# A table of due times, x of the first batch through DRAM, low k in three and more products of zeros in a pooled-attention and two-MLP kernel

## The chip, the cores and the metric

The kernel runs on one core of one Trainium2 chip. The metric is the device time of one execution in microseconds (us). Lower is better. The engines are PE (matmul; PEld is its weight load), DVE, ACT, POOL (GpSimd) and SP, which issues nearly all DMAs; each works through its own list of instructions in order.

## The reference

All arrays are float32. Queries are averaged in pairs (1152 to 576), then 16 heads (2 batches of 8) attend to 1152 keys, and two MLPs follow over the 1152 pooled tokens.

```python
q_pool = q.reshape(B, H, S // factor, factor, D).mean(axis=3)      # (2, 8, 576, 64)
scores = scale * np.matmul(q_pool, k.transpose(0, 1, 3, 2))        # (2, 8, 576, 1152)
attn = np.exp(scores - np.max(scores, axis=-1, keepdims=True))
attn = attn / (np.sum(attn, axis=-1, keepdims=True) + 1e-09)
x = np.matmul(attn, v)                                             # to (1152, 512)
h = x @ w_in;  x = np.maximum(0.01 * h, h) @ w_out                 # 512 -> 2048 -> 512
h = x @ w_in2; x = (h / (1.0 + np.exp(-h))) @ w_out2               # 512 -> 2048 -> 512
```

## The kernel before, in words

**Precision.** A matmul operand is a sum of a rounded high part (fp32r, made by a copy on ACT) and a low part (value minus high, a subtraction, mostly on POOL). A product of two such operands is three matmuls: high by high, low by high, high by low. q, k, x, the weights and the hidden g are all split in this way.

**Attention** (`attention`) goes over 8 pairs of heads, four of each batch. For a pair, `load` and `load_v` issue the DMAs of k, q and v (`L455`), POOL adds the two rows of q (`L498`), ACT makes the high parts (`L501`, `L504`) and POOL the low ones (`L507` for q, `L510` for k, all 1152 columns of k in one instruction). Twelve `max_tile`s and two `rest_tile`s (`L579`, `L611`) are products of the high parts alone; DVE reduces them to row maxima (`L586`, `L615`), which go into a row of one matmul operand. Of the first pair that row is made by PE and ACT (`first_rows`: `L632`, `L644`, `L651`), of the others by small DMAs `row<-mn`. `scores` makes 18 tiles (two column halves of 256 and 320, nine key tiles each) with four terms each (`L708`), the last of which subtracts the maximum; ACT takes the exponential (`L714`). `sum_up` adds the exponentials tile by tile (`L752`), most on DVE and the others on POOL; `pv` multiplies by v (`L766`); `sums` (`L804`) adds over partitions on PE, and the factors 1/sum come back over DRAM. `norm` multiplies x by them (`L893`) and splits it into xh and xl. Of pairs 4, 5, 6 that is deferred to the start of the second stage (`defer=3`; `L901`, `L904`, `L905`), and the last pair has a path of its own (`end`: `L852`, `L861`, `L865`, `L872` to `L874`).

**At the start** PE runs 18 products of zeros (`warm`, `L951`) and 6 more behind each of the first six max tiles (`warm_between=3`, two matmuls each). They only occupy PE.

**MLPs** (`mlps`) take the tokens in two groups (512 and 640) and the hidden units in four blocks. The first block of layer one is made plainly (`layer_in_plain`, `L1311`); all others by `cell`, seven products of half size in place of eight (`L1357`), which needs differences of quarters of x: `transform` makes them on DVE (`L1215`) from x in 32 bits and splits them on ACT and POOL (`L1229`, `L1235`). Since attention leaves only xh and xl, `rebuild` first adds the two again on POOL (`L1251`, eight additions). `layer_out_t` (`L1432`) and `layer_out` (`L1498`) are the second matmuls. `rectify` makes g (`L1284`, `L1289` on ACT, `L1279` on POOL). Weights come by `wraw` DMAs (`L168`), are converted on ACT and DVE (`L192` to `L231`) and split (`L239`, `L243`).

**The order of the work** is the program's own: each stage is a list of tasks with an engine, a weight (planned us), a due time and the tasks they wait for. `Plan.run` plays a schedule: an engine that is free takes the ready task with the smallest rank, and instructions are emitted in that order. Due times came from formulas with the numbers in `PARAMS`. In `attention` the rank also had `stay_mode` and `stay_port`, which put off a task that would change PE's mode (scores and v products load the array differently) or meet a taken DVE/POOL port:

```python
def rank(self, t, now):
    stay = PARAMS["stay_mode"] if t["mode"] else PARAMS["stay_port"]
    return t["due"] + stay * (self.cost(t, now) - t["weight"]), t["n"]
```

## Time and profile before

| | us |
|---|---|
| median of 3 runs (lowest to highest) | 612.25 (610.78 to 613.85) |
| the profiled execution's own time | 612.46 |
| its span in the profile | 610.3 |
| PE, PEld busy in the span | 589.1 (97%), 506.1 (83%) |
| DVE, ACT, POOL busy in the span | 503.0 (82%), 334.9 (55%), 364.6 (60%) |
| mean granted PE clock | 0.986 |

A matmul is shown busy from its start until its modelled end, so overlapping matmuls and waits inside a group count as busy. How fast PE goes is read from how many products a stretch holds. The profiled execution lies 0.2 us above the median of the runs. 2.2 us of its time lie around the span.

### The profile page before, as it was taken

The numbers are of one execution on the slowest core, as the hardware profiler recorded it, in microseconds if no ns is written. First come the engines' busy times: TensorE is split into PE (matmuls) and PEld (weight loads), VectorE is DVE, ScalarE is ACT, GpSimd is POOL, SyncE is SP. The second block draws the span as 40 slices with busy tenths as digits, with TensorE's granted clock in tenths as the row PEclk, the third lists the DMA queues.
The fourth block names the chain that finished last, engine by engine and source line by source line (L and its number), as shares of the span: only waits on it lengthen the run. The fifth ranks groups of instructions, "written<-read, shape, count | busy, mean of one in ns | idle before, by whom it ended". The sixth has DMA issues, their size and how long they took to land.

```text
span 610.3 us, 11499 instructions
## 1 busy us (share of the span) xinstructions
PE 589.1 (97%) x4420; PEld 506.1 (83%) x4420; DVE 503.0 (82%) x797; ACT 334.9 (55%) x573; POOL 364.6 (60%) x251
## 2 busy tenths in 40 slices
PE   7898999999999989699999999999999999999997
PEld 5776686686777759599899999899889998998986
DVE  5699898888987997968989898898878898888633
ACT  3556575585575554666455563756666655545410
POOL 6937576667562249995555464878946546437400
PEclk9599999999999999989999999999999999999999
DMA  8022443355132113233233233222232333233012
GB/s 285 25 79 61 113 111 93 98 143 178 22 96 76 56 35 94 79 104 101 73 105 104 69 104 104 70 70 69 68 106 76 101 101 104 74 100 105 0 70 86
DMA packets 33119, 55.06 MB, mean 90 GB/s; under 512 B 13197, under 2 KB 14633, under 8 KB 33065
## 3 DMA queue, kind: packets, MB, share of 16 engines
q1 hardware_dynamic: 32920, 54.14, 28.8%
q8 instruction: 34, 0.56, 0.4%
q10 hardware_dynamic: 144, 0.20, 0.1%
q14 instruction: 21, 0.16, 0.1%
HBM read 49.81 MB, written 2.42 MB: 86 GB/s over the span
## 4 chain that ended last, share of the span: by engine, by line
PE 77%; POOL 8%; DVE 8%; issue 3%; ACT 3%; DMA 1%; SPq 0%; ACTq 0%; DVEq 0%; POOLq 0%
PE psum L1357 24%; PE psum L1498 16%; PE psum L708 12%; PE psum L1432 12%; PE psum L766 8%; DVE late L752 3%; PE psum L579 3%; POOL tl L1235 2%; PE psum L1311 1%; ACT e L714 1%; POOL late L1251 1%; PE psum L611 1%; DVE mx L586 1%; POOL xl L1235 1%; POOL xl L1467 1%
## 5 line engine op out<-in xcount | busy, mean ns | idle before, releaser
L1432 PE MATMUL psum<-g,wout 128*128 128x320 f32 (+1 forms) x576 | 104.8, 340 | 3.6 <-ACT acc L1449 3.2
L1432 PEld LDWEIGHTS psum<-g,wout 128*128 128x128 f32 x576 | 93.4, 191 | 12.0 <-ACT acc L1449 4.0
L1498 PE MATMUL psum<-wout,g 128*128 128x512 f32 (+1 forms) x444 | 100.6, 384 | 0.0
L714 ACT ACTIVATE e<-psum 128x512 f32<-128x512 f32 (+1 forms) x144 | 89.2, 655 | 19.7 <-PE psum L708 17.3
L586 DVE TENSOR_REDUCE mx<-psum 128x2 f32<-128x768 f32 x96 | 87.8, 949 | 9.7 <-PE psum L579 7.4
L1498 PEld LDWEIGHTS psum<-wout,g 128*128 128x128 f32 x444 | 81.1, 188 | 15.8
L1381 DVE TENSOR_TENSOR late<-psum,late 128x256 f32<-128x256 f32 (+3 forms) x84 | 54.6, 654 | 21.2 <-PE psum L1357 15.5
L766 PE MATMUL psum<-e,vnat 128*64 128x320 f32 (+1 forms) x576 | 71.6, 407 | 0.0
L752 POOL TENSOR_TENSOR late<-late,e 128x512 f32<-128x512 f32 (+1 forms) x37 | 52.4, 1417 | 31.5 <-DVE late L752 26.7
L752 DVE TENSOR_TENSOR late<-late,e 128x640 f32<-128x640 f32 (+1 forms) x73 | 66.1, 941 | 1.4 <-POOL late L752 0.3
L243 POOL TENSOR_TENSOR wout<-wt,wout 128x512 fp32r<-128x512 f32 x32 | 42.0, 1313 | 39.6 <-ACT wout L239 39.5
L1279 POOL TENSOR_TENSOR g<-a,g 128x512 fp32r<-128x512 f32 (+1 forms) x34 | 49.6, 1472 | 24.5 <-ACT a L1289 24.4
L766 PEld LDWEIGHTS psum<-e,vnat 128*64 128x64 f32 x576 | 40.7, 137 | 28.0 <-ACT e L714 1.4
L243 POOL TENSOR_TENSOR w<-wt,w 128x896 fp32r<-128x896 f32 (+1 forms) x18 | 36.7, 2038 | 31.4 <-ACT w L239 29.4
L1279 POOL TENSOR_TENSOR g<-late,g 128x512 fp32r<-128x512 f32 (+1 forms) x28 | 40.0, 1437 | 18.2 <-ACT late L1289 10.5
L708 PE MATMUL psum<-qh,kh 64*128 64x320 f32 (+1 forms) x288 | 50.0, 343 | 0.7 <-ACT e L714 0.3
L196 DVE TENSOR_SCALAR psum<-psum 128x512 f32<-128x512 f32 x59 | 40.7, 692 | 11.4 <-ACT psum L192 11.1
L1357 PE MATMUL psum<-xh,w 128*128 128x256 f32 (+1 forms) x224 | 49.5, 296 | 0.2 <-ACT late L1395 0.2
L243 POOL TENSOR_TENSOR more<-wt,more 128x896 fp32r<-128x896 f32 x14 | 30.4, 2173 | 30.4 <-ACT more L239 27.9
L1357 PE MATMUL psum<-xh,more 128*128 128x256 f32 (+1 forms) x224 | 48.5, 293 | 0.0
L708 PE MATMUL psum<-row,onesr 64*128 64x320 f32 (+1 forms) x288 | 43.7, 299 | 0.0
L708 PE MATMUL psum<-qh,kl 64*128 64x320 f32 (+1 forms) x288 | 43.6, 298 | 0.0
(129 smaller groups left out, 1378.9 us busy)
## 6 DMA issues: line engine op xcount, KB each, us to landing
wraw<-in_moe_w_in_dram SPq DMA_DIRECT2D x32, 512.0 KB, 4.0
wraw<-in_moe_w_out_dram SPq DMA_DIRECT2D x32, 512.0 KB, 3.3
vnat<-in_v_dram SPq DMA_DIRECT2D x8, 576.0 KB, 5.7
knat<-in_k_dram SPq DMA_DIRECT2D x7, 576.0 KB, 5.3
qnat<-in_q_dram SPq DMA_DIRECT2D x7, 576.0 KB, 6.4
out_dram<-acc SPq DMA_DIRECT2D x8, 256.0 KB, 2.0
xl<-late SPq DMA_DIRECT2D x7, 288.0 KB, 4.8
xh<-d SPq DMA_DIRECT2D x14, 144.0 KB, 3.8
```

The lines of the kernel that those rows point to most:

```text
L196: nc.vector.tensor_scalar(out=tf, in0=tf, scalar1=2.0, scalar2=W_TOP, op0=ALU.max, op1=ALU.min)
L243: self.nc.gpsimd.tensor_tensor(out=lo, in0=tf, in1=hi, op=ALU.subtract)
L586: nc.vector.tensor_reduce(out=mx[p][:, u, c], in_=ps[:, :, 0:KC], op=ALU.max, axis=AX.X)
L708: nc.tensor.matmul(out=ps[:, j, 0:n], lhsT=lhsT[own[j], :], rhs=rhs[own[j], cs], start=m == 0, stop=m == len(terms) - 1)
L714: nc.scalar.activation(out=e_t[h, t], in_=ps[:, :, 0:n], func=ACTF.Exp, scale=scale)
L752: e.tensor_tensor(out=a, in0=e_t[h, 0] if t == 1 else a, in1=e_t[h, t], op=ALU.add)
L766: nc.tensor.matmul(out=vps[h][0][own[j], 0, 0:CW[c]], lhsT=vnat[p][:, j, t, :], rhs=e_t[h, t][:, j, :], start=(t == 0), stop=(t == NKT - 1),)
L1279: (nc.vector if fast else nc.gpsimd).tensor_tensor(out=gl, in0=a(), in1=gh, op=ALU.subtract)
L1357: nc.tensor.matmul(out=box[key][:, bank, 0:n], lhsT=w[:, i, :], rhs=y, start=(kk == 0 and q == 0), stop=(kk == 1 and q == 2),)
L1381: nc.vector.tensor_tensor(out=to, in0=p, in1=y, op=ALU.add)
L1432: nc.tensor.matmul(out=box[x][:, c, 0:n], lhsT=wt[:, ms], rhs=y[:, c * n:(c + 1) * n], start=(f == 0 and y is gh and wt is oh), stop=(f == ...
L1498: nc.tensor.matmul(out=box[x][:, c, 0:n], lhsT=y[:, ts], rhs=wt[:, cs], start=(f == 0 and y is gh and wt is oh), stop=(f == FB - 1 and y i ...
```

## The change

1. **Due times from a table.** `DUES` holds a due time for each task of both stages; `Plan.add` takes it in place of the formula's. The rank's penalties are set to 0, and the port of DVE and POOL is now counted in the MLP stage too.
2. **x in 32 bits is kept.** `rebuild` is gone. x of the first batch (pairs 0 to 3) is written to a DRAM tile `kept` when it is normalized and comes back by two DMAs (`fetch`, one for each token group). x of the second batch is normalized straight into `acc1`, where `transform` reads it. All of pairs 4 to 6 is still done in the second stage.
3. **Loads in order.** k and q of the second pair are loaded ahead of v.
4. **Low k in three.** k's low part is made in three instructions of 384 columns.
5. **More products of zeros.** They follow nine of the first pair's max tiles in place of six, and three more (six matmuls) follow the first row of maxima.
6. Planned weights and lags are altered; ACT copies the two halves of a v product in a fixed order; the five POOL additions of the last pair are other ones.

```diff
+DUES = {
+    name: [int(x) / 100 for x in text.split()] for name, text in dict(attention="""
+0 50 300 0 130 110 280 62 0 193 62 124 186 248 53 402 437 566 601 969 1069 691 1152 626 769 524 591 678 869 981 1242
...
+        if self.dues:
+            t["due"] = self.dues[t["n"]]
...
-    load1=10.25,
+    load1=-5.0,
...
-    v=-15.94,
-    v0=-6.44,
+    v=-13.5,
+    v0=8.0,
...
-    last_pool=((1, 0), (1, 1), (2, 0), (5, 0), (6, 0)),
+    last_pool=((1, 0), (1, 1), (2, 1), (3, 0), (8, 0)),
...
+    warm_tiles=9,
+    warm_rows=3,
...
-    stay_mode=129.57,
-    stay_port=42.33,
+    stay_mode=0.0,
+    stay_port=0.0,
...
-        y = two("k_low", 1.27, due[2], lambda e: k_low(p, every, e), after=[y], give=("knat",))
         for i in range(NQ):
-            out["kl", i] = [y]
+            out["kl", i] = [two("k_low", 0.45, due[2], lambda e, i=i: k_low(p, chunks[i], e), after=[y])]
+        add("-", 0.0, 0.0, after=sum((out["kl", i] for i in range(NQ)), []), give=("knat",))
...
+        idle = P["warm_between"] if p == 0 and NQ * u + c < P["warm_tiles"] else 0
...
-            if p == 0:
-                warm(P["warm_between"] if u < 2 else 0)
+            warm(idle)
...
+        if idle:
+            add("PE", 0.215 * idle, due, lambda: warm(idle), order=[t], mode="rows")
...
+        def later(p):
+            x = place(whole, p)
+            return (
+                p % HP,
+                lambda e: e.tensor_tensor(out=x, in0=place(xl, p).bitcast(F32), in1=place(xh, p).bitcast(F32), op=ALU.mult),
...
+        keep = dma(due, lambda: (kept[p], flat()), after=made, lag=P["lag"])
...
-    def rebuild(g, after):
-        made = []
+    def fetch(g):
+
         held, at = whole(0, g)
...
+        lo, hi = (0, groups[1][0]) if g == 0 else (groups[1][0], NT // 2)
+        to = held[:, :, lo:hi]
+        return [add(
+            "SP", 0.5, -100.0, lambda: nc.sync.dma_start(out=to, in_=kept[:, :, lo:hi].rearrange("k p n -> p k n")),
+            after=end_made[:1] if g == 0 else [], lag=5.0,
+        )] + (all_made if g else [])
```

**How instructions move.** At the start of SP's list, before (`vnat` is v, `knat` k, `qnat` q; the 128x1152 loads are those of pairs 1 and 2):

```order
L455 DMA qnat<-in_q_dram 128x2x320
L455 DMA vnat<-in_v_dram 128x2x576 x2
L455 DMA knat<-in_k_dram 128x1152
L455 DMA qnat<-in_q_dram 128x1152
L455 DMA knat<-in_k_dram 128x1152
```

and in the change:

```order
L605 DMA qnat<-in_q_dram 128x2x320
L605 DMA knat<-in_k_dram 128x1152
L605 DMA qnat<-in_q_dram 128x1152
L605 DMA vnat<-in_v_dram 128x2x576
L605 DMA knat<-in_k_dram 128x1152
L605 DMA qnat<-in_q_dram 128x1152
L605 DMA vnat<-in_v_dram 128x2x576
```

Both v loads moved from ahead of the second pair's k and q to behind them, and behind those of the third pair.

On PE, at the end of the first pair, before (`L766` is the product with v, `L804` the sums, `L611` and `L579` the second and third pair's maxima):

```order
L766 MATMUL psum<-e_94,vnat 64x256 x18
L766 MATMUL psum<-e_95,vnat 64x320 x18
L611 MATMUL psum<-kh,rest_92 128x384 x3
L804 MATMUL psum<-late,ones 32x288 x4
L579 MATMUL psum<-kh,qh 128x384 x2
```

and in the change (`L923`, `L963`, `L765`, `L734` in the same roles):

```order
L734 MATMUL psum<-kh,qh 128x384 x2
L923 MATMUL psum<-e_97,vnat 64x256 x12
L734 MATMUL psum<-kh,qh 128x384 x4
L923 MATMUL psum<-e_97,vnat 64x256 x6
L923 MATMUL psum<-e_98,vnat 64x320 x18
L765 MATMUL psum<-kh,rest_95 128x384
L963 MATMUL psum<-late,ones 32x288 x4
```

Max tiles now stand between the v products. Up to the first product of the MLPs, PE's list changes between the three kinds (scores and maxima; v products; rests, sums and the rest) 27 times before and 58 times in the change.

On POOL, from the fourth low part of g on, before (`L1251` is `rebuild`, `L1279` makes g's low parts, `L1235` those of the differences, `L243` those of weights):

```order
L1251 TENSOR_TENSOR acc_2685<-xh,xl 128x640 x2
L243 TENSOR_TENSOR wout_2692<-wt,wout_2692 128x512
L1251 TENSOR_TENSOR late<-xh,xl 128x512 x2
L243 TENSOR_TENSOR more<-wt,more 128x896
L1251 TENSOR_TENSOR late<-xh,xl 128x512 x2
L1235 TENSOR_TENSOR tl<-acc_2685,th 128x2x320 x2
```

and in the change (`L1398` is the old `L1235`, `L1438` the old `L1279`, `L392` the old `L243`):

```order
L392 TENSOR_TENSOR wout_2736<-wt,wout_2736 128x512
L1398 TENSOR_TENSOR tl<-acc_2730,th 128x2x320
L392 TENSOR_TENSOR wout_2737<-wt,wout_2737 128x512
L1438 TENSOR_TENSOR g_2745<-a,g_2745 128x640
L1398 TENSOR_TENSOR tl<-acc_2730,th 128x2x320
L1398 TENSOR_TENSOR tl<-late,th 128x2x256
```

All eight additions are gone from POOL's list, and the low parts of g stand between those of the differences, no longer behind all of them.

## Rows read from the trace of the kernel before

**Rows 1.** Stretches: length, busy us of PE, PEld, DVE, ACT, POOL; PEclk, DMA, GB/s.

```profile
6.84:50.34 43.50, 38.40 (x317) 28.73 (x315) 36.32 (x47) 22.08 (x42) 30.22 (x21) 0.84 0.34 111
17.60:31.20 13.60, 13.44 (x86) 11.24 (x88) 8.96 (x13) 7.60 (x17) 13.30 (x9) 0.50 0.01 1
50.50:192.90 142.40, 140.89 (x1505) 104.62 (x1509) 127.30 (x175) 87.27 (x149) 88.61 (x58) 1.00 0.36 101
212.15:275.85 63.70, 55.72 (x308) 47.56 (x307) 53.85 (x81) 36.19 (x62) 53.15 (x33) 0.97 0.24 75
300.00:400.00 100.00, 100.00 (x657) 95.65 (x656) 88.05 (x162) 52.83 (x90) 56.45 (x38) 1.00 0.30 95
418.00:442.00 24.00, 22.52 (x166) 21.77 (x164) 19.16 (x30) 16.64 (x28) 20.88 (x15) 1.00 0.22 65
```

**Rows 2.** Timeline of the first pair: start, length, engine, what, and what ended idle time.

```profile
3.96 1.11 SPq L455 DMA_DIRECT2D vnat<-in_v_dram  x2
13.40 0.15 DVE L632 TENSOR_REDUCE xh<-mx 128x4 fp32r<-128x12 f32 x1
15.19 1.39 POOL L498 TENSOR_TENSOR qnat<-qnat 128x576 f32<-128x576 f32 x1 [3.49 <-DMA qnat<-in_q_dram]
16.62 0.68 ACT L501 ACTIVATE qh<-qnat 128x576 fp32r<-128x576 f32 x1 [1.73 <-POOL qnat L498]
17.21 0.36 ACT L651 ACTIVATE row<-psum 128x256 fp32r<-128x256 f32 x1
45.33 5.01 DVE L752 TENSOR_TENSOR late<-late,e 128x640 f32<-128x640 f32 x2
```

**Rows 3.** Chain that ended last, inside two pairs: start, length, engine, what.

```profile
112.85 8.88 PE psum L766 x72
...
122.36 0.72 PE psum L611 x3
...
152.80 0.47 PE psum L708 x8
...
159.02 0.17 PE psum L579 x2
159.20 0.59 PE psum L708 x8
```

**Rows 4.** Timeline of DVE and POOL where a sum met k's low part, and DVE alone.

```profile
94.49 3.06 DVE L752 TENSOR_TENSOR late<-late,e 128x640 f32<-128x640 f32 x1
93.90 2.97 POOL L510 TENSOR_TENSOR kl<-knat,kh 128x1152 fp32r<-128x1152 f32 x1 [3.33 <-ACT kh L504]
212.28 0.81 DVE L752 TENSOR_TENSOR late<-late,e 128x640 f32<-128x640 f32 x1
```

**Rows 5.** Groups by shape, POOL: count, then busy us, mean ns.

```profile
L510 POOL TENSOR_TENSOR kl<-knat,kh 128x1152 fp32r<-128x1152 f32 x7 | 20.0, 2853 | 3.3 <-ACT kh L504 3.3
L510 POOL TENSOR_TENSOR kl<-knat,kh 128x384 fp32r<-128x384 f32 x3 | 3.0, 1011 | 0.7 <-ACT kh L504 0.7
L1251 POOL TENSOR_TENSOR late<-xh,xl 128x512 f32<-128x512 f32 x4 | 6.8, 1714 | 0.0
L1251 POOL TENSOR_TENSOR acc<-xh,xl 128x640 f32<-128x640 f32 x4 | 6.3, 1580 | 0.0
```

**Rows 6.** Chain that ended last, handover and after: start, length, engine, what.

```profile
267.07 8.78 PE psum L1432 x58
...
302.78 6.14 PE psum L1357 x42
...
386.35 10.91 PE psum L1432 x48
```

**Rows 7.** Timeline of DVE and POOL in the handover.

```profile
227.83 0.80 DVE L872 TENSOR_TENSOR late<-late,psum 128x288 f32<-128x288 f32 x2
229.16 0.92 DVE L874 TENSOR_TENSOR xl<-late,xh 128x288 fp32r<-128x288 f32 x2
265.44 3.12 POOL L1279 TENSOR_TENSOR g<-a,g 128x640 fp32r<-128x640 f32 x2
```

More of the change, by code (lines that the diff above doesn't have):

```diff
@@ L391, in cost @@
             w += self.SWITCH[t["mode"]]
-        if t["port"]:
-            w += max(0.0, self.port - now)
         return w
@@ L450, in attention, with dma @@
     at = lambda h: T0 + h * U
-    def dma(due, out_in, after=(), order=(), take=(), lag=None, begin=0.0, queue="SP"):
+    def dma(due, out_in, after=(), order=(), take=(), lag=None, begin=0.0, queue="SP", w=None):
         def go():
@@ L675, in dve @@
                 rest_max(p, slice(0, 128), mn[p][:, 0, len(units):])
-        t = add("DVE", 0.1 + 0.1 * c, due, dve, after=maxima)
+        t = add("DVE", 0.22 + 0.1 * c, due, dve, order=maxima)
         for u in us + (len(units),) * c:
@@ L793, in go @@
             banks.give(i)
-        return add("ACT", 0.28 + 0.05 * c, due, go, after=[after], take=() if c else ("pvs",), give=("duo",))
+        first = [box["evac", p]] if c else []
+        box["evac", p] = x = add("ACT", 0.28 + 0.05 * c, due, go, after=[after], order=first, take=() if c else ("pvs",), give=("duo",))
+        return x
     def sums(p, after, due):
@@ L1049, in mlps @@
 @with_exitstack
-def mlps(ctx, tc, xh, xl, weights, banks, out, end, late_t):
+def mlps(ctx, tc, xh, xl, weights, banks, out, end, late_t, kept):
     nc = tc.nc
@@ L1294, in rectify @@
         ready = [y, z]
-        done[u, f] = ready + [add("DVE", 0.07 + n / 860, d, low, after=ready) if fast else add("POOL", wp, d, low, after=ready)]
+        done[u, f] = ready + [add("DVE", 0.07 + n / 860, d, low, after=ready, port=True) if fast else add("POOL", wp, d, low, after=ready)]
     def layer_in_plain(x):
@@ L1529, in pair_end @@
     def pair_end():
-        (sums, copy, factors, spread, give), steps, later = end()
+        (sums, copy, factors, spread, give), steps, later = end(acc1)
         d = P["end"]
@@ L1545, in pair_end @@
             a, b = P["norm_on"]
-            cost = dict(DVE=0.8, POOL=1.45)
-            x = add(a, cost[a], x, lambda norm=norm: norm(on[a]), after=[], order=before, begin=begin)
+            cost = dict(DVE=0.72, POOL=1.42)
+            x = add(a, cost[a], x, lambda norm=norm: norm(on[a]), order=before, begin=begin, port=True)
             y = add("ACT", 0.58, d, high, after=[x])
-            z = add(b, cost[b], d, lambda low=low: low(on[b]), after=[y])
+            z = add(b, cost[b], d, lambda low=low: low(on[b]), after=[y], port=True)
             normed[k] = [y, z]
@@ L1555, in mlps @@
     all_made = end_made + sum(normed.values(), [])
+    fetched = [fetch(g) for g in range(2)]
     transformed = {}
```

118 lines of the change are left out of this document (57 added, 61 removed), and 138 rows, old and new, of the table DUES.

## The prediction

> **What bounds the kernel now.** I read the busy time by stretch first, since the stages have different limits. From 300 to 400 us PE is busy for 100.00 of 100.00 us [rows 1]: there PE is the bound, a better order can win nothing, and any new wait costs its full length. In three other stretches PE loses time. In the first pair of heads (6.84 to 50.34) DVE is busy for 36.32 of 43.50 us, and within it, from 17.60 to 31.20, PE is busy for 13.44 of 13.60 us at a granted clock of 0.50, the lower of its two levels, 1.2 GHz. Over the next six pairs (50.50 to 192.90, from the first pair's sums to the seventh's) PE and DVE are both nearly full. In the handover (212.15 to 275.85) the chain and the timeline show PE behind POOL. I went on to the chain that ended last for the pace of PE alone, to the timeline for single waits, and to the groups by shape for POOL's durations.
>
> **The first pair: 5.5 us.** Three parts act here: loads in order, products of zeros, order by table. *Loads:* the first row of maxima is ready in DVE at 13.40 + 0.15 = 13.55, but ACT copies it at 17.21, behind the second pair's q, which waits for POOL, which waited 3.49 us for a DMA [rows 2]. That DMA stood behind two v loads issued at 3.96; in the change they come later. The row still has q's pooling (1.39) ahead of it, so I put it at about 15.0: 2.2 us earlier. *Clock:* PE fell to half speed after a stretch in which it had little to do, and 13.44 us of work at half speed are 6.7 us at full speed. The added dummy products fill that stretch. They cost PE nothing if they hold the clock, since PE waited there for DVE's reductions. *DVE* sets the earliest end: of its 36.32 us, the last two additions took 5.01 where one alone takes 0.81 [rows 2, 4], so 3.4 us are waiting, and 32.9 us from 6.84 end at 39.8, which is 10.6 us before 50.34. The bounds are thus 2.2 (only the loads help) and 10.6. I take 5.5: the 6.7 of the clock is the nearest, less a little because exponentials on ACT pace the scores once PE is fast.
>
> **The six full pairs: 6.0 us.** One takes 142.40 / 6 = 23.7 us. PE's own work in it, at the pace of the chain [rows 3], is 8.88 (v products) + 9 x 0.47 + 9 x 0.59 (score tiles) + 12 x 0.17 (max tiles) + 0.72 (rest), and as much again for the sums: 21.9. So 1.8 per pair is lost, 11.0 in six. DVE's busy time is 127.30 / 6 = 21.2, of which some is waiting: a sum that met k's low part on POOL took 3.06 in place of 0.81 [rows 4], and such sums are on the chain. In the change the next pair's maxima are spread into the v products and the sums stand later, so that PE need not wait for DVE's last addition. Against that, PE changes its kind of product 58 times in place of 27. The trace shows no such change by itself; the bounds are 0 (a max tile between scores takes its own 0.17) and 0.2 (three rest products behind v products take 0.72, three at 0.17 would take 0.51). I take 0.1, or 2.4 us for the some 24 added in six pairs; at 0.2 it is 4.8. Low k in three: POOL holds the port for 3 x 1.011 in place of 2.853 [rows 5], but an addition that comes in the middle waits for one piece. The Trainium skill (SBUF — State Buffer, Who interferes with whom) says that a DVE instruction with two SBUF inputs and a GpSimd instruction that reads SBUF exclude each other for the whole instruction, the one that begins first winning. The 3.06 agrees. By that rule alone additions that come one after another can meet each piece in turn, and this part would be worth nothing; the sum would then be about 2 us smaller. I take -1.0 per pair net of the changes of kind: 6.0, between -4.8 (changes at 0.2, nothing won) and +11.0.
>
> **The handover: 8.0 us.** PE's products from 212.15 to 275.85 are 96 of 512 columns at 10.91 / 48 = 0.227 and 192 of 320 at 6.14 / 42 = 0.146 [rows 6], plus two small sums at 0.72: 51.3 us in a stretch of 63.70, so 12.4 are lost. POOL is busy for 53.15 of it [rows 1] and its last two low parts of g begin only at 265.44 [rows 7], just ahead of PE's next run at 267.07 [rows 6]. The eight additions that go are 6.8 + 6.3 = 13.1 us of POOL [rows 5]. Their place is taken by two DMAs: the second group's needs 64 columns per row and is read long before; the first group's can start only after PE's last sum, 48 x 0.227 = 11 us behind the last v product, and its differences are needed when the other 40 us of PE's 51.3 are done, so I cost it at nothing; if that cover went, PE would wait for the whole transfer. The four writes to DRAM stand in SP's list among the last pair's row DMAs; what is queued behind them waits until the norm is done, 2 to 3 us that the scores of the pair before hide. What is late next: DVE, busy for 53.85 us, ends 9.85 below 63.70; and with the table only 18 products stand between the last sums and their factors, after which PE needs the last pair's x: 227.83 to 230.08, 2.25 us [rows 7]. 9.85 less most of 2.25 gives 8.0. The bounds are 12.4 (all) and 4 (weight loads that now stand behind the fetch in SP's list come late).
>
> **The turn between the layers: 0.5 us**, from 0 to 1.5: PE is idle for 24.00 - 22.52 = 1.5 us there [rows 1], and the table lets some products of the second matmul in ahead. The other edits (fixed order of two copies, five other POOL additions, planned weights) change no work and are in the terms above. The end of the program is as it was.
>
> **The sum.** 5.5 + 6.0 + 8.0 + 0.5 = 20.0 us, against the profiled execution's 612.46, which is 0.2 above the median: 592.5 us.
>
> **Rivals.** *The pairs win nothing.* PE is at most 1.8 us per pair above its own work, and every added change of kind eats from that. For it speaks that PE is busy for 140.89 of 142.40 us, against it the 3 us waits of DVE on the chain. Then 612.46 - 14.0 = 598.5. *The dummy products do not hold the clock*, so that they do not do what they are there for: the first term falls to 2.2, 595.8 us. For it: the clock fell although 54 such products had run. By the Trainium skill (TensorE: Matmul & The Clock Gate, What's actually happening) the clock is held back by default and activity releases it; this trace does not bear that out alone, since PE was busy for 13.44 of 13.60 us and stayed at 0.50. By that rule the saving would be the smaller one, and this rival's 595.8 holds. *The handover turns over to DVE or late weights:* the third term is 4, 596.5 us; with a loss of 1% in the 330 us of MLPs where PE has no slack now, about 600. *Slower:* POOL and DVE meet more often. Place: DVE's nine additions per pair, once the table spreads POOL's shorter pieces among them and the rank no longer avoids a taken port. Price: up to 2.25 us for each meeting [rows 4]. DVE has 23.7 - 21.2 = 2.5 us free per pair; beyond that each us is on the path. To end 3 us slower, the pairs must lose 17 us where they were to win 6, about 2.9 per pair, so 5.4 us more waiting in DVE: between two and three more such meetings per pair. That gives about 616 us. The pieces are shorter than before, which speaks against it.
>
> **How the numbers follow.** Half a per cent, 3 us, is about what a measurement of this kernel can tell from no change. Forecast (587 to 597) 0.47; pairs win nothing 0.18; clock not held 0.11; handover or MLPs short 0.10; better than 587, with two terms near their upper bounds, 0.04; two or more rivals at once, 604 to 609, 0.02; within 3 us of now 0.04; slower 0.04. Faster is the sum of all but the last two, 0.92. The range of 582 to 603 takes in the first four, single rivals at their bounds and most of the better case; it leaves out about 0.15, the last three and the best end of the better case among it.
>
> **What would show it.** Right: a granted clock of 1.00 from 17 to 31 us, the first sums at about 45 in place of 50.5, sums 22.7 us apart, the first product of the MLPs near 200, POOL free of additions and the last plain second products (the 58 of 267.07) ending some 55 us behind that product. Wrong: additions of 1.5 us and more in every pair, a DVE without idle time in the handover, PE waiting for x read from DRAM, or PE below 99 of 100 us between the turn of the stages and that of the layers.

## The result and the profile after

| | before | after |
|---|---|---|
| median (lowest to highest), 4 runs each | 612.39 (610.78 to 613.85) | 604.71 us (603.04 to 607.19) |
| ratio to before, with its interval | | 0.9879 [0.9831, 0.9926] |
| the profiled execution, its span | 612.46, 610.3 | 607.19, 605.3 us |
| mean granted PE clock | 0.986 | 1.000 |

The kernel is faster by 7.7 us, not by 20. Measured again beside the first experiments, the changed kernel took 606.97 us (6 runs), a ratio of 0.9934 [0.9914, 0.9953], a gain of about 4; the two intervals overlap. The profiled execution of after lies 2.5 us above its median, so the accounting below is of a gain of 5.0 us in the span.

Busy time by stretch of the changed kernel. The columns are those of [rows 1]; the stretches are the first pair up to its sums, the 13.6 us of low clock in before, first sums to last v product, first product of the MLPs to first `cell` product, the MLPs, and the turn of the layers with what lies beside it.

```profile
6.84:45.23 38.39, 35.12 (x336) 25.39 (x336) 32.32 (x45) 20.22 (x38) 26.46 (x23) 1.00 0.37 122
17.60:31.20 13.60, 11.89 (x130) 9.16 (x126) 11.13 (x17) 9.43 (x21) 13.10 (x12) 1.00 0.13 40
45.23:211.33 166.10, 162.09 (x1728) 118.49 (x1727) 146.14 (x200) 100.16 (x178) 102.18 (x72) 1.00 0.36 104
211.63:268.18 56.55, 51.92 (x302) 45.76 (x301) 44.81 (x71) 33.07 (x58) 39.39 (x24) 1.00 0.31 96
300.00:400.00 100.00, 100.00 (x663) 96.06 (x662) 87.78 (x161) 55.70 (x93) 59.09 (x40) 1.00 0.31 95
400.00:434.00 34.00, 31.89 (x218) 29.99 (x217) 30.73 (x44) 21.52 (x36) 28.84 (x21) 1.00 0.21 63
```

The same view of before over first sums to last v product, a stretch that the rows ahead of the prediction cut otherwise:

```profile
50.49:211.79 161.30, 159.79 (x1725) 119.42 (x1725) 142.52 (x194) 100.73 (x173) 93.77 (x61) 1.00 0.34 98
```

The marks come from the groups of PE's sums, before (`L804`) and after (`L963`): count, duration in ns, first and last start.

```profile
L804 PE MATMUL psum<-late,ones x56: 402/406/430, 50.5 to 193.1; 128*32 128x288 f32 x56
```
```profile
L963 PE MATMUL psum<-late,ones x56: 402/406/430, 45.2 to 204.3; 128*32 128x288 f32 x56
```

The last sums stand later among the products than before, so they are no mark of progress; the last v product is, and it starts at 211.33 in place of 211.79. The 5.3 us won in the first pair are gone when attention ends:

| stretch | before | after | won | forecast |
|---|---|---|---|---|
| start to first sums | 50.49 | 45.23 | +5.26 | +5.5 |
| first sums to last v product | 161.30 | 166.10 | -4.80 | +6.0 |
| last v product to first product of the MLPs | 0.36 | 0.30 | +0.06 | |
| to the first `cell` product, as the chain that ended last dates it | 63.70 | 56.55 | +7.15 | +8.0 |
| to the end of the span | 334.5 | 337.1 | -2.6 | +0.5 |

Next, what PE waited for from first sums to last v product. Columns: engine, tile and line that waited, what it waited for, us in total, times, longest. Before:

```profile
PE psum L804 <- DVE late L752: 2.2, 2, 1.7
PE psum L708 <- ACT e L714: 0.3, 1, 0.3
PE psum L579 <- DVE mx L586: 0.3, 1, 0.3
PE psum L708 <- DVE mx L586: 0.2, 1, 0.2
```

After (`L765` makes rests, `L865` scores, `L740` reduces maxima, `L909` adds exponentials):

```profile
PE psum L765 <- DVE mx L740: 1.2, 1, 1.2
PE psum L865 <- DMA row<-mn: 0.9, 1, 0.9
PE psum L865 <- DVE mx L740: 0.7, 2, 0.4
PE psum L963 <- DVE late L909: 0.4, 1, 0.4
...
```

The sums wait 0.4 us for DVE's last addition, no longer 2.2. But of these 2.2 us the longest wait, 1.7, ends with the very product that opens the stretch, so it belongs to the first pair:

```profile
50.49 0.69 PE L804 MATMUL psum<-late,ones 128*32 128x288 f32 x8 [1.68 <-DVE late L752]
```

In the stretch itself the sums' wait went from 0.6 to 0.4 us, and what I credited the table with was hardly there to be won. Before, PE stood still for 161.30 - 159.79 = 1.5 us of the whole stretch, and its waits after the first product were 1.3. After, it stands still for 4.0, and all waits are 3.9, in eight places, most of which did not wait before.

The losses are not spread evenly. From the last v product of one pair to that of the next, the third pair takes 25.3 us and the sixth 25.2, where `e10_combined` below, whose first pair ends within 0.4 us of the same time, takes 23.4 and 24.0; no other pair differs by more than 0.7. The largest wait stands in the third pair, from the timeline of all engines of the changed kernel:

```profile
85.94 6.09 DVE L909 TENSOR_TENSOR late<-late,e 128x512 f32<-128x512 f32 x4
86.52 3.00 POOL L664 TENSOR_TENSOR kl<-knat,kh 128x384 fp32r<-128x384 f32 x2
89.49 1.85 POOL L652 TENSOR_TENSOR qnat<-qnat 128x576 f32<-128x576 f32 x1
91.95 0.94 DVE L740 TENSOR_REDUCE mx<-psum 128x2 f32<-128x768 f32 x1
92.95 0.45 PE L765 MATMUL psum<-kh,rest 128*128 128x384 f32 x1 [1.19 <-DVE mx L740]
```

Four additions, 0.69 us each where nothing meets them, 2.76 together, took 6.09, beside two pieces of k's low part and the pooling of q on POOL, back to back. The maxima behind them came late, and PE waited 1.19 us.

In the handover, the chain that ended last, after (before's ran through POOL's additions and low parts up to [rows 7]):

```profile
227.27 7.37 DMA wraw<-in_moe_w_in_dram
234.66 0.65 ACT psum L341
...
238.78 6.43 PE psum L1591 x27
...
268.18 1.39 PE psum L1516 x12
269.57 0.88 PE psum L1591 x6
```

POOL is out of it, as forecast (39.39 us busy in place of 53.15). In its place stands a weight load of 7.37 us. SP's list shows what it stands behind, the fetch of x (`L1413`):

```profile
225.88 0.37 SPq L1413 DMA_DIRECT2D late<-kept  x1
227.27 0.38 SPq L317 DMA_DIRECT2D wraw<-in_moe_w_in_dram  x1
```

PE waits 4.6 us in this stretch (56.55 - 51.92): 2.2 at 238.8, in the chain that the weight load leads, and nearly as much earlier, for a tile that ACT makes (`L1448`). ACT had stood idle for 6.31 us up to 218.85, by the profile for a DMA of the seventh pair's factors:

```profile
222.16 0.50 PE L1470 MATMUL psum<-xh,w 128*128 128x512 f32 x1 [2.08 <-ACT a L1448]
218.85 0.63 ACT L388 ACTIVATE wout<-wt 128x512 fp32r<-128x512 f32 x1 [6.31 <-DMA d<-cmp]
```

### The profile page after: what moved, and what is told of

Read it like the earlier page. It is cut to its first block, busy times and chain, and to the rows that moved or that the text cites. A ratio compares the mean times of both kernels' runs of the same rounds, so it can differ in the third digit from the quotient of the medians.

```text
span 605.3 us, 11529 instructions
## 1 busy us (share of the span) xinstructions
PE 586.3 (97%) x4444; PEld 500.5 (83%) x4444; DVE 495.3 (82%) x797; ACT 331.9 (55%) x573; POOL 358.0 (59%) x257
## 4 chain that ended last, share of the span: by engine, by line
PE 77%; DVE 10%; DMA 4%; ACT 3%; issue 3%; POOL 2%; SPq 1%; DVEq 0%; ACTq 0%; POOLq 0%
PE psum L1516 24%; PE psum L1657 16%; PE psum L1591 16%; PE psum L865 10%; PE psum L923 6%; DVE late L909 3%; DVE mx L740 3%; PE psum L734 2%; ACT e L871 2%; DMA wraw<-in_moe_w_in_dram 1%; DMA knat<-in_k_dram 1%; PE psum L1470 1%; DVE wt L360 1%; DMA row<-mn 1%; DMA d<-cmp 1%
## 5 line engine op out<-in xcount | busy, mean ns | idle before, releaser
L1591 PE MATMUL psum<-g,wout 128*128 128x320 f32 (+1 forms) x576 | 102.8, 336 | 2.2 <-ACT a L1448 2.2
L740 DVE TENSOR_REDUCE mx<-psum 128x2 f32<-128x768 f32 x96 | 88.1, 952 | 19.5 <-PE psum L734 11.8
L1657 PE MATMUL psum<-wout,g 128*128 128x512 f32 (+1 forms) x444 | 103.2, 385 | 0.4 <-DVE a L1540 0.2
L1591 PEld LDWEIGHTS psum<-g,wout 128*128 128x128 f32 x576 | 92.0, 188 | 9.5 <-ACT a L1448 2.5
L871 ACT ACTIVATE e<-psum 128x512 f32<-128x512 f32 (+1 forms) x144 | 86.0, 657 | 19.3 <-PE psum L865 17.5
L909 POOL TENSOR_TENSOR late<-late,e 128x512 f32<-128x512 f32 (+1 forms) x37 | 53.9, 1457 | 34.6 <-DVE late L909 22.5
L923 PE MATMUL psum<-e,vnat 128*64 128x256 f32 (+1 forms) x576 | 73.2, 408 | 0.0
L392 POOL TENSOR_TENSOR wout<-wt,wout 128x512 fp32r<-128x512 f32 x32 | 43.0, 1348 | 42.9 <-ACT wout L388 42.7
L923 PEld LDWEIGHTS psum<-e,vnat 128*64 128x64 f32 x576 | 40.0, 137 | 28.8 <-issue 1.5
L1438 POOL TENSOR_TENSOR g<-a,g 128x512 fp32r<-128x512 f32 (+1 forms) x34 | 50.8, 1503 | 20.7 <-ACT a L1448 18.4
L909 DVE TENSOR_TENSOR late<-late,e 128x640 f32<-128x640 f32 (+1 forms) x73 | 61.4, 881 | 0.6
L392 POOL TENSOR_TENSOR w<-wt,w 128x896 fp32r<-128x896 f32 (+1 forms) x18 | 39.2, 2178 | 34.1 <-ACT w L388 31.0
L1438 POOL TENSOR_TENSOR g<-late,g 128x512 fp32r<-128x512 f32 (+1 forms) x28 | 39.9, 1436 | 26.6 <-ACT late L1448 25.1
L1516 PE MATMUL psum<-xh,w 128*128 128x256 f32 (+1 forms) x224 | 50.5, 296 | 1.6 <-ACT late L1554 1.6
L865 PE MATMUL psum<-qh,kh 64*128 64x320 f32 (+1 forms) x288 | 48.1, 329 | 2.3 <-DVE mx L740 1.2
L392 POOL TENSOR_TENSOR more<-wt,more 128x896 fp32r<-128x896 f32 x14 | 29.8, 2133 | 26.8 <-ACT more L388 20.7
L341 ACT ACTIVATE psum<-wraw 128x512 f32<-128x512 f32 x59 | 36.9, 626 | 15.8 <-DMA wraw<-in_moe_w_out_dram 10.2
L865 PE MATMUL psum<-row,onesr 64*128 64x320 f32 (+1 forms) x288 | 42.9, 292 | 0.9 <-DMA row<-mn 0.9
```

The lines of the kernel that those rows point to most:

```text
L392: self.nc.gpsimd.tensor_tensor(out=lo, in0=tf, in1=hi, op=ALU.subtract)
L740: nc.vector.tensor_reduce(out=mx[p][:, u, c], in_=ps[:, :, 0:KC], op=ALU.max, axis=AX.X)
L865: nc.tensor.matmul(out=ps[:, j, 0:n], lhsT=lhsT[own[j], :], rhs=rhs[own[j], cs], start=m == 0, stop=m == len(terms) - 1)
L871: nc.scalar.activation(out=e_t[h, t], in_=ps[:, :, 0:n], func=ACTF.Exp, scale=scale)
L909: e.tensor_tensor(out=a, in0=e_t[h, 0] if t == 1 else a, in1=e_t[h, t], op=ALU.add)
L923: nc.tensor.matmul(out=vps[h][0][own[j], 0, 0:CW[c]], lhsT=vnat[p][:, j, t, :], rhs=e_t[h, t][:, j, :], start=(t == 0), stop=(t == NKT - 1),)
```

## The experiments

I tested two theories. A: the parts of the change work as forecast, each by itself, and the order of the table costs the pairs what they lose. B: the order as such is not it; single meetings of DVE and POOL, and late DMAs, at places where lists that were planned against one clock drift apart, cost it. Ratios are to before, timed on the same chip. Of each edit the main lines are shown, some joined into one; `...` marks a cut. Pairs are counted from one here, from zero in the expectations of `e5_klow_on_dve` and `e11_v_first`. An edit that changes planned weights or due times makes the program draw up its lists anew; where this moved other work than the edit names, the text says so.

**Is it the table?** `a_again` is the changed kernel itself, measured again.

> The changed kernel once more, with nothing edited, as the measure for the other runs and for a second profile: 603 to 607 us by either theory. Theory A (the order): the first pair's gain is real, and the table's order loses it again in the six full pairs by waits of its own. Theory B (a common bound): something other than the order paces the attention, so that it ends near 211 us whatever the first pair does. Both expect the first product of the MLPs within 2 us of 211.9.

It took 606.97 us, 0.9934 [0.9914, 0.9953]; first sums 45.1, last v product 211.65, first `cell` product 267.28.

`e1_attention_before` has attention in the order of before, with low k whole and the dummies of before; x kept, the fetches and the MLPs' table are the change's.

```diff
-    load1=-5.0, v=-13.5, v0=8.0, stay_mode=0.0, stay_port=0.0
+    load1=10.25, v=-15.94, v0=-6.44, stay_mode=129.57, stay_port=42.33
...
-    plan = AttentionPlan(DUES.get("attention", ()))
+    plan = AttentionPlan(())
...
```

> Attention in the order of before (no table, loads, dummy products and low k as before), with x of the first batch through DRAM and the MLPs of the change. Theory A and theory B both expect the handover's gain alone, 7.4 us off 612.4: 605.0, with the first product of the MLPs at 211.8. If it is above 608, the order of the attention is worth more than the profiled execution showed; if it is below 603, the change of the attention costs time.

It took 608.02 us, 0.9945 [0.9922, 0.9968], and its last v product starts at 211.3. So all that the change does to attention is worth nothing at attention's end. The time is 3 us above what both theories expected. In the first pair its lists are those of before, instruction by instruction, and yet its first sums come at 49.0 in place of 50.5: two profiles of one order differ by 1.5 us there.

`e6_before_order_klow3` is that kernel with low k in three pieces.

```diff
...
-        y = two("k_low", 1.27, due[2], lambda e: k_low(p, every, e), ...)
+            out["kl", i] = [two("k_low", 0.45, due[2], lambda e, i=i: k_low(p, chunks[i], e), after=[y])]
```

> Attention in the order of before but with k's low part in three, and the MLPs of the change: beside the run with the order of before (608.0). If low k in three is by itself worth the 6.7 us that it was worth under the table, it comes to 601 to 603. If its worth there was only that the table was made for pieces, it stays within 1.5 us of 608.

It took 604.92 us, 0.9893 [0.9869, 0.9917], between the two expectations: first sums at 46.6 (49.0 in `e1_attention_before`), last v product at 208.1, a stretch of 161.6. The pieces alone win 2.4 us in the first pair, where the order is otherwise the same, and in the rules' order none of it is lost again.

`e12_attention_rules` drops only attention's table: the rules of before order the tasks, with the change's loads, dummies and pieces.

```diff
-    stay_mode=0.0, stay_port=0.0
+    stay_mode=129.57, stay_port=42.33
-    plan = AttentionPlan(DUES.get("attention", ()))
+    plan = AttentionPlan(())
```

> The change with the attention ordered by the rules of before (its table dropped, both penalties for staying restored); loads, dummy products, low k in three, x through DRAM and the MLPs by table stay as in the change. Theory A3 (the table's order is what loses the six pairs: DVE has the same 148 us of work between the first sums and the last v product, but stands idle for 18.5 us in place of 13.4): first sums near 45, the last v product 161 to 163 us behind them, attention ends at 206 to 208, and the time is 3 to 6 us below the change. Theory B (what the first pair wins is lost in the pairs by whatever order): attention ends at 210 to 212 and the time stays within 1.5 us of the change.

It took 609.94 us, 0.9979 [0.9954, 1.0005], above what either theory expected: first sums at 47.1 and last v product at 211.6, where the table's is and theory B had it. Its stretch between the two is 164.5 us, 1.6 less than with the table and 3.0 more than in `e6_before_order_klow3`, which has the loads, dummies, planned weights, ACT's copies and POOL's additions of before. So the table is not the whole cause: the rules lose time too once these numbers are the change's. One place holds nearly all of it. DVE, then POOL, in that kernel's timeline, and all of its conversions of this kind (count, shortest, median and longest in ns):

```profile
152.52 4.16 DVE L345 TENSOR_SCALAR wt<-wt 128x512 f32<-128x512 f32 x1
```
```profile
151.05 1.32 POOL L392 TENSOR_TENSOR w<-wt,w 128x512 fp32r<-128x512 f32 x1
152.31 1.31 POOL L909 TENSOR_TENSOR late<-late,e 128x512 f32<-128x512 f32 x1
153.57 1.61 POOL L909 TENSOR_TENSOR late<-e 128x640 f32<-128x640 f32 x1
155.12 1.27 POOL L909 TENSOR_TENSOR late<-late,e 128x512 f32<-128x512 f32 x1
```

```profile
L345 DVE TENSOR_SCALAR wt<-wt x5: 414/420/4162, 138.1 to 214.1; 128x512 f32<-128x512 f32 x5
```

A conversion of weights that takes 0.42 us alone took 4.16: it ended at 156.68, 0.29 us after the last of POOL's instructions. The maxima behind it came late, and PE waited 2.5 us for them at 157.6. That pair, the sixth, takes 2.9 us more than in `e6_before_order_klow3` (26.9 and 24.0).

**The first pair.** `e2_dummies_as_before` leaves out the added dummies.

```diff
-            warm(idle)
+            warm(idle if NQ * u + c < 6 else 0)
...
-            add("PE", 0.215 * idle, due, lambda: warm(idle), ...)
+            add("PE", 0.215 * idle, due, lambda: None, ...)
```

> The change without the dummy products that it adds (three tiles' worth and those behind the first row); the order stays. Theory A: the clock falls to 0.50 again from about 18 us on, the first sums come at 48 to 51 in place of 45.2, and the time is 3 to 6 us above that of the change. Theory B: the first pair is as late, but the attention ends within 1 us of the change, and so does the program. If the clock stays at 1.00, the added dummy products were not what holds it, and nothing moves.

It took 607.13 us, 0.9942 [0.9916, 0.9968], as the change does; first sums at 46.0, 0.9 later, with the clock at 0.92 and not at 0.50.

`e4_before_dummies` adds such dummies to the kernel before.

```diff
-                warm(P["warm_between"] if u < 2 else 0)
+                warm(P["warm_between"] if u < 3 else 0)
...
+            if not c:
+                warm(3)
```

> The kernel before with the added dummy products alone. By the prediction's first term the clock stays at 1.00 from 17 to 31 us and PE does 13.4 us of work in 6.7 less: the first sums at 44 to 47 in place of 50.5 and the time at 605 to 608. If PE then waits for DVE or POOL in that stretch, as in the change, the clock is held and the time falls by 1 to 3 us only.

It took 609.22 us, 0.9973 [0.9954, 0.9992], by the ratio some 1.7 us less than before; first sums at 49.1. That is 1.4 earlier than in the profile of before, but no earlier than in `e1_attention_before`, which has no such dummies.

`e3_klow_whole` makes k's low part in one instruction, by its planned weight; the lists that came of it are not the change's.

```diff
-            out["kl", i] = [two("k_low", 0.45, due[2], lambda e, i=i: k_low(p, chunks[i], e), after=[y])]
+            out["kl", i] = [two("k_low", 0.0 if i else 1.27, due[2],
+                lambda e, i=i: None if i else k_low(p, every, e), after=[y] if not i else out["kl", 0])]
```

> The change with k's low part in one piece, at the place of the first piece. If the pieces hurt because additions of DVE that follow each other meet each piece in turn (four additions that took 6.09 us from 85.94 on), it is 1 to 3 us faster than the change. If they help, as the prediction had it, single additions of about 3 us come back and it is 1 to 3 us slower. Theory B: within 1 us.

It took 613.67 us, 1.0059 [1.0033, 1.0085], 6.7 us above `a_again`, where 1 to 3 were expected. Its first sums come at 51.3, but this mark has moved: 200 score products stand ahead of them in place of 144. The last v product of the first pair stands at 44.3 (43.5 in `a_again`), that of the third at 99.8 (94.3), the last of attention at 219.9 (211.7), so half of the loss falls in the third pair and little in the first. As all five lists differ, the loss is not the pieces' alone.

`e11_v_first` puts both v loads back ahead of the second pair's k and q, as before, and leaves every other list alone. (In the change the first v load stands behind the second pair's k and q, the second one behind the third pair's.)

```diff
+    go = {n: plan.tasks[n]["emit"] for n in (33, 179, 314)}
+    plan.tasks[314]["emit"] = lambda: (go[33](), go[179](), go[314]())
+    plan.tasks[33]["emit"] = plan.tasks[179]["emit"] = None
```

> The change with both first v loads ahead of pair 1's k and q, as before; all other lists as they are. If the order of the loads is what brought the first pair forward, the first sums come 2 to 3 us later than the change's 45.1 and the time rises by 1 to 3 us. If not, both stay within 1 us.

It took 609.41 us, 0.9979 [0.9962, 0.9996]; first sums at 50.1, 5.0 later than in `a_again` and twice what was expected. The pairs behind them take 166.5 us, as in the change (166.1 and 166.6): whenever the first pair ends, the table's order takes the same time.

The stretch that ran at 0.50 before [rows 1], in `e1_attention_before`, `e2_dummies_as_before`, `e4_before_dummies`, `e11_v_first` and `e6_before_order_klow3`:

```profile
17.60:31.20 13.60, 13.01 (x106) 10.66 (x108) 9.55 (x14) 9.18 (x21) 13.52 (x9) 0.68 0.01 2
```
```profile
17.60:31.20 13.60, 12.16 (x126) 9.88 (x124) 10.60 (x16) 8.74 (x19) 12.57 (x11) 0.92 0.04 16
```
```profile
17.60:31.20 13.60, 12.94 (x112) 10.54 (x114) 9.55 (x14) 8.89 (x20) 13.21 (x9) 0.75 0.00 0
```
```profile
17.60:31.20 13.60, 11.81 (x107) 8.82 (x105) 9.23 (x13) 8.26 (x17) 12.24 (x12) 0.88 0.12 43
```
```profile
17.60:31.20 13.60, 13.46 (x116) 10.96 (x116) 10.35 (x15) 9.55 (x20) 12.47 (x11) 0.71 0.00 1
```

The last figure but two is the clock. Against the first sums, in the same order: 0.68 and 49.0, 0.92 and 46.0, 0.75 and 49.1, 0.88 and 50.1, 0.71 and 46.6. Across kernels with different lists the two do not go together. Where the lists are alike, or alike but for dummies, they do, by little: from 0.50 to 0.68 (before and `e1_attention_before`) the sums come 1.5 us earlier, from 0.92 to 1.00 (`e2_dummies_as_before` and `a_again`) 0.9, and from 0.71 to 1.00 (`e6_before_order_klow3` and `e10_combined` below) 1.2. Nowhere do they come to 6.7 us. DVE stands behind the clock: in before, in `e1_attention_before` and in `e4_before_dummies` alike the first sums wait 1.68 us for DVE's last addition.

So in the change's order the loads carry the first pair: taken back alone they lose 5.0 us, where the whole change had won 5.3.

**The pairs.** `e5_klow_on_dve` moves the low parts of k of pairs 4 to 8 from POOL to DVE, some 7 us of work in DVE's list.

```diff
-lambda e, i=i: k_low(p, chunks[i], e)
+lambda e, i=i: k_low(p, chunks[i], nc.vector if p > 2 else e)
```

> The change with k's low part of pairs 3 to 7 issued on DVE, at the same places of the program; the order on PE, ACT and SP is the change's. Theory A1 (meetings): the table keeps POOL's pieces and DVE's additions apart, but on the chip the additions run 4 us later against the table than the pieces, so that they meet; the four additions at 86 to 92 us that took 6.3 us go back to 3.0, DVE gets 15 pieces of some 0.5 us, and as the long additions of 1.4 to 2.8 us go, the time falls by 1 to 4 us. Theory A2 (DVE is full): the 15 pieces, 7 us in all, lie on the path and the time rises by 3 to 7 us.

It took 610.60 us, 1.0003 [0.9980, 1.0025]; the stretch from first sums to last v product grew from `a_again`'s 166.6 to 171.4. `e15_no_weight_steps` does the opposite and leaves 15 of DVE's weight steps out:

```diff
-                    eng, w, due, step, port=m > 0, ...
+                    eng, w, due, None if 0 < m < 4 else step, port=m > 0, ...
```

> The change with three of the four DVE steps of the five weight slices left out that stand among the pairs (limits, shift and sign; the weights of the first products are then not the reference's): 15 DVE instructions, 10.1 us, go from 120 to 205 us, all other lists stay. Theory A4 (DVE sets the pace of the pairs, so that work moved to it there costs 0.7 us per us, as in the run with 7 us more): the last v product comes 160 us behind the first sums in place of 166.5, and the time is 5 to 8 us below the change. Theory B2 (PE's own list and the waits for transfers set it): the stretch shortens by less than 2 us.

It took 605.59 us, 0.9886 [0.9856, 0.9915], and the stretch:

```profile
45.40:210.74 165.34, 162.02 (x1727) 118.46 (x1727) 139.72 (x185) 99.90 (x177) 98.05 (x71) 1.00 0.36 105
```

With 15 instructions less to do, DVE mostly idles more, 165.34 - 139.72 = 25.6 us against 20.0 in the change, and the stretch is 0.8 us shorter than in the change's first profile (1.2 against `a_again`). So in the change it is not the amount of DVE's work that binds. That it is the place of the work, as the 4.9 us of `e5_klow_on_dve` suggest, these two runs alone do not show.

`e9_sp_two_places` changes only SP's list, at two places where a late DMA was seen: pair 5's loads of k and q go behind two row copies, so that its low parts come later on POOL, and a weight load that waits for its buffer goes behind the last row copy.

```diff
...
+    behind(750, 490)
+    behind(751, 490)
+    behind(1182, 776)
```

> The change with two places of SP's list exchanged and every other list as it was: pair 5's k and q are loaded behind the next two row copies in place of ahead of them (they are not needed before 118 us), and a weight load that waits for a free buffer stands behind the last row copy of that pair in place of ahead of it (140 us). Theory A1 (single places where lists that run at their own pace meet): the four additions at 86 to 92 us take 3 to 4 us in place of 6.3, PE's losses from 90 to 100 us (3.6 us) and from 140 to 150 us (2.1) shrink by 2 and 1, and the time falls by 2 to 4 us. Theory A2 (DVE is full everywhere, single places do not matter): what is won there is lost again within the next pair, and the time stays within 1 us of the change.

It took 605.00 us, 0.9904 [0.9883, 0.9925], by the ratios 0.3% or 1.8 us less than `a_again`, with intervals that overlap; the stretch is 165.2, 1.4 less than in `a_again`. Both places moved as meant, and the third pair takes 23.9 us (25.4 in `a_again`); the sixth still takes 25.1 (25.6). The four additions, against 6.09:

```profile
86.31 3.24 DVE L909 TENSOR_TENSOR late<-late,e 128x512 f32<-128x512 f32 x4
```

SP's list in the change, then in this kernel:

```profile
137.17 1.80 SPq L605 DMA_DIRECT2D row<-mn  x3
140.43 0.33 SPq L317 DMA_DIRECT2D wraw<-in_moe_w_in_dram  x1
140.81 0.47 SPq L605 DMA_DIRECT2D row<-mn  x1
```
```profile
136.33 2.44 SPq L605 DMA_DIRECT2D row<-mn  x4
139.59 0.57 SPq L317 DMA_DIRECT2D wraw<-in_moe_w_in_dram  x1
```

In the change the fourth row copy stood behind a load that was not issued until 140.43, and the scores of `L865` waited 0.9 us for `row<-mn`; here all four go at once.

**The handover.** `e7_fetch_later` lets one weight load go ahead of the fetch.

```diff
-            after=end_made[:1] if g == 0 else [], lag=5.0,
+            after=end_made[:1] if g == 0 else [], lag=5.0, begin=0.0 if g else 14.0,
```

> The change with the fetch of the first group (1 MB) issued behind the first weight load in place of ahead of it. If the fetch and that load share the DMA engines, the load lands in 4 us in place of 6 to 7, PE's wait of 2.2 us near 236 us shrinks, and the time falls by 1.5 to 2.5 us. If the load was late for its buffer alone, nothing moves (within 0.7 us).

It took 606.55 us, 0.9919 [0.9894, 0.9944], by the ratios 0.9 us less than `a_again`, with intervals that overlap. SP's list, and ACT's first use of that weight:

```profile
226.27 0.38 SPq L317 DMA_DIRECT2D wraw<-in_moe_w_in_dram  x1
226.75 0.42 SPq L1413 DMA_DIRECT2D late<-kept  x1
```
```profile
231.20 0.62 ACT L341 ACTIVATE psum<-wraw 128x512 f32<-128x512 f32 x1 [0.57 <-DMA wraw<-in_moe_w_in_dram]
```

Issued ahead of the fetch, the load is used 4.9 us later; behind it, 7.4 (5.9 in `a_again`). From the start of the first MLP product to that of the first `cell` product it is 52.2 us (by these marks 56.4 in the change and 55.3 in `a_again`). The fetch's place does not explain all of that. PE's wait at 238.8, 2.2 us in the change and 0.4 in `a_again`, is 0.25 here, but the other one, at 222.2, is gone too, and so it is in kernels that leave the fetch where it is. Of these `e9_sp_two_places` and `e11_v_first` take 52.5 us; there the load is used 5.7 us after its issue.

`e8_mlps_no_table` takes the MLPs' table away.

```diff
-    plan = Plan(P["starts"], DUES.get("mlps", ()))
+    plan = Plan(P["starts"], ())
```

> The change with the MLPs ordered by their rules, not by the table; attention is the change's. If the table is what lets products of the second matmul in at the handover, the last plain second products end 58 to 64 us behind the first product of the MLPs in place of 56, and the time rises by 2 to 6 us. If the table costs the MLPs their 2.5 us (the layer turn lost 3.8 us against 2.4 before), the time falls by 1 to 3 us.

It took 620.11 us, 1.0130 [1.0098, 1.0162], with 70.1 us in that stretch: some 12 us above `a_again` by the ratios, where 2 to 6 were expected at most. Ordered by the rules with the change's numbers, x in 32 bits wins nothing here.

**A version that beats both.** `e10_combined` joins `e6_before_order_klow3`, the dummies of `e4_before_dummies` and the fetch of `e7_fetch_later`.

> The best parts together: attention in the order of before with k's low part in three and the change's dummy products, the MLPs of the change, and the fetch behind the first weight load. If the dummy products hold the clock at 1.00 in that order too, PE's stretch of some 9 us at 0.50 is 4 us shorter, the first sums come at 43 to 45 in place of 46.6, and with 1 to 3 us from the fetch the time is 598 to 602. If the clock there does not matter, as in the change's order (0.9 us), it is 602 to 604.

It took 599.53 us (599.07 to 601.85), 0.9824 [0.9806, 0.9842], as expected, 1.1% below `a_again` by the ratios and with the intervals apart; the change's first, wider interval begins at 0.9831. First sums to last v product, the stretch of low clock, and the handover:

```profile
45.30:206.93 161.63, 160.47 (x1725) 119.41 (x1725) 148.27 (x202) 102.31 (x176) 101.78 (x71) 1.00 0.38 106
17.60:31.20 13.60, 12.43 (x138) 9.96 (x134) 11.57 (x17) 10.42 (x21) 13.24 (x12) 1.00 0.00 1
207.29:259.22 51.93, 51.46 (x301) 45.68 (x299) 44.16 (x70) 32.67 (x57) 37.99 (x24) 1.00 0.35 108
```

It has the first pair of the change and the pairs of before, and PE is busy for all but 0.5 us of the handover. `e14_combined_loads` gives it the change's loads as well.

```diff
-    load1=10.25, v=-15.94, v0=-6.44
+    load1=-5.0, v=-13.5, v0=8.0
```

> The best version so far (attention in the order of before, low k in three, the added dummy products, the fetch behind the first weight load; 599.5) with the first loads in the order of the change as well. If the order of the loads brings the first sums forward by 2 to 5 us here too, as it did in the change's order (50.1 to 45.1), and the pairs keep their pace of 23.9, the time is 595 to 598. If DVE is already what sets the first pair, the first sums stay at 45 and the time at 599 to 601.

It took 608.97 us, 0.9960 [0.9936, 0.9984], which neither expectation had: last v product at 215.9, 9 us later, 8 of which are lost by the last v product of the second pair. (Its first sums, at 55.8, stand behind 216 score products in place of 144.) The loads that the table's order could not do without cost this one 9 us, by way of the lists that the rules drew up around them: about a quarter of PE's products stand elsewhere. It is not the loads alone: `e12_attention_rules`, with the same loads and the change's planned weights, has its first sums at 47.1.

## Why the prediction was wrong

The sign was right, the time was not: 604.71 us lies above the upper end of the range, 603.

**The six pairs are the step that failed:** "So 1.8 per pair is lost, 11.0 in six", of which I took 1.0 per pair as winnable by the order. The 11 us are the difference between PE's time and a pace that I had put together from the shortest rows of each kind [rows 3]. The first row of that stretch that I should have asked is PE's idle time, 1.5 us, or the list of its waits, 1.3 without the one ahead of the first sums. The rest is lengthening of single steps. I add up the steps from one product's start to the next, less the usual shortest one of each kind. Steps that are no more than 0.25 us too long come to 16.1 us before, 16.7 after and 17.0 in `e10_combined`, so no order tried here has won on them. The waits that an order could win were thus worth 1.5 us, not 11.

That the pairs came out at -4.8, my lower bound, is luck. The bound stood for changes of kind at 0.2 with nothing won. By the same sum longer steps went from 2.6 to 6.3 us, two more rests and the like took 0.6, and the short ones 0.5 net: 23 more changes of kind, at 0.1 each as I had taken them, were nearly made up by shorter steps ahead of scores (10.7 and 8.1). So the loss is in waits, which the bound did not have.

**The rival that lost time was not borne out as it stood.** I had put POOL and DVE meeting more often at 616 us, from meetings in every pair. They do not meet more often: over what they take alone (0.69 and 0.82 us), DVE's additions from first sums to last v product lost 10.2 us before, 8.1 after and 10.5 in `a_again`. What counts is where a meeting falls. What I had set against the pieces with the Trainium skill (SBUF — State Buffer, Who interferes with whom), that additions in a row can meet each piece in turn, is what happened at 85.94 in the change: four additions met two pieces and the pooling. It cost 6.09 - 2.76 = 3.3 us of DVE, of which PE saw 1.19. Where the lists drifted apart is shown too: at pair 5 the low parts of k came 1.2 us behind the table's planned times, the additions 5, so what the table had planned one after the other met. `e9_sp_two_places` undid that place and one late DMA, `e12_attention_rules` has another meeting. That drift explains all of the pairs' loss is not shown; against `e10_combined` about 1 us of 4 lies outside the third and sixth pair, and I could not put it down to single places. Theory B fits the places that were found, theory A that the table's order took 166 to 167 us wherever its lists were left as they are; both may hold a part.

**The first pair: 5.26 for 5.5, for other reasons, so by luck.** That "the 6.7 of the clock is the nearest" failed. The clock was held at 1.00, so the rival in which it is not did not come, yet without the added dummies, at 0.92, the first sums came 0.9 us later, and where lists are alike the clock is worth 0.9 to 1.5 us. In the change's order the loads did the work: 5.0 us, where I had put them at 2.2. PE's half speed was mostly hidden behind DVE, which my own upper bound named as the next limit. Next to nothing is left of it at the end of attention in the change; in `e10_combined` it is, 211.79 - 206.93 = 4.9 us.

**The handover: 7.15 for 8.0.** POOL came free as forecast, and DVE was not next (44.81 of 56.55). Six second products of 0.88 us now stand behind the mark, so fairly it is 6.3. What is short are two waits of PE. One, 2.2 us (0.4 in `a_again`), is the weight load behind the fetch, the lower bound's reason; the fetch itself, "I cost it at nothing", brought x in time. The other, 2.1 us behind ACT (1.8 in `a_again`), was in no term. Without both, `e7_fetch_later` and `e10_combined` take 52.2 and 51.9 us, so with the six products taken off 10.4 to 10.7 of 63.5 us (the same marks before) are won, near the upper bound of 12.4. What makes the second wait come and go was not tested, nor is it shown how much of the 4 us the fetch's place alone is worth.

**The rest: -2.6 us for +0.5.** PE idles 34.00 - 31.89 = 2.1 us around the turn of the layers, against 1.5 in [rows 1]: no gain. The six products above are 0.9. For the other 1.1 us, with PE at 100.00 of 100.00 us as before, I have no place; steps too short for the trace's waits are all that is left, and that was not tested.

## What to carry to other kernels

Before an order is credited with a gain, read the idle time and the waits of the engine it is to speed up, and see on which side of the stretch's first product a wait lies; a pace put together from best rows shows time that no order tried here could win. An order from a table holds within the clock it was planned by, so look for streams that drift apart (lists paced by DMAs against lists paced by PE), and for a load that waits for its buffer ahead of something urgent. Parts of a replanned order don't add up: undo each in place, and try the parts again in the old order, where here low k in three and the dummies, with x kept and its fetch moved, made the best version. When an edit makes a program replan, compare the lists first: a mark like the first sums can move without any time being lost.

## What the runs showed of the hardware

A DVE instruction that waits for POOL can wait through several: 0.42 us of work took 4.16 beside three POOL instructions back to back and ended 0.29 us behind the last of them. The Trainium skill (SBUF — State Buffer, Who interferes with whom) says that conversions of this sort can use the port pair shared with GpSimd and are then shut out for the whole of one GpSimd instruction; the trace agrees, and goes further in that the wait did not end when that one did.

A load whose DMA was issued behind a large one on the same queue lands later. The same weight load was used 7.4 us after its issue in the change (5.7 to 8.3 in the eleven profiles with the fetch right ahead of it) and 4.5 to 4.9 in the three with the fetch behind it. The Trainium skill (DMA: Bandwidth & Descriptors, Queues, rings and completion order) says that each DMA engine takes what one queue gives it in ring order, which agrees; no run here put the two on different queues, and what moves the time between 5.7 and 8.3 stays open.

PE's clock in one stretch of 13.6 us ran from 0.50 to 1.00 over these kernels. With equal lists, 0.68 in place of 0.50 went with an end of the stage 1.5 us earlier; between kernels with other loads or other low parts of k the two did not go together (0.88 and 50.1 us, 0.71 and 46.6).
